# Layer statistics on TensorE: each 32-column block sums its own 128 tokens, turned within PSUM, without a fold

## Chip, cores, metric

One core of a Trainium2 chip. The metric is device time in microseconds (us), where smaller is better. A run counts as slow when it is over 1.5% above the fastest run of the same kernel; all comparisons of times below use fast runs.

The engines go by these names: PE is TensorE (matmul), PEld its weight loads, DVE is VectorE, ACT is ScalarE, POOL is GpSimd, SP is SyncE. PSUM is where TensorE writes its results, in banks. The granted clock is the share of TensorE's full clock that it gets. A column tile is a strip of 32 of TensorE's 128 columns that is used as a small unit with its own weights; how TensorE is split for a group of matmuls is its tiling mode.

## The reference

```python
kv  = einsum('bhsd,bhse->bhde', k, v)          # 8 batches, 8 heads, 576 tokens, 64
o   = einsum('bhsd,bhde->bhse', q, kv)
x   = o / sqrt(mean(o*o, -1) + 1e-6) * g_norm  # -> 4608 tokens x 512
h   = x @ w_in                                 # 512 -> 1024
u   = h * exp(h) / sum(exp(h))                 # the maximum that it subtracts cancels out
out = (u - mean(u)) / sqrt(var(u) + 1e-6) * g_ln @ w_out
```

The mean and the variance of `u` are over the 1024 features of one token. The kernel keeps features on partitions, so these sums run across partitions, and it does them on TensorE.

## The kernel before

The tokens are taken in nine chunks (0 to 8) of 512. Per chunk the kernel makes `h` (8 groups of 4 matmuls), `e = exp(h)` on ACT, `u = h*e` on DVE, `usq = u*u` on POOL or ACT, `es` (sums of pairs of `e`) on POOL, then three sums per token, from them the factor `rstd`, and `out` (8 groups of 4 matmuls), which DVE scales by `rstd` into `ob` and SP stores. The attention part of later batches (kv, qT, o, s) lies in between.

These are the parts concerned:

```python
banks = {"h": 2, "out": 2, "o": 2, "s": 1, "misc": 1}          # PSUM banks by name

def sums(c, part):                       # 20 matmuls of 512 columns on four 32-column tiles
    if part == 0:
        T["sum", c] = bank(("misc" if c else "h", "sum", c), [128, 512], FP32)
    i, src = ((1, T["u", c]), (0, T["usq", c]), (2, T["es", c]))[part]
    n_src = NF // 2 if part == 2 else NF
    for n in range(n_src):
        j = n % 4
        nc.tensor.matmul(
            T["sum", c][32 * j:32 * j + 32, :], stat_sel[:, i, :], src[:, n, :],
            start=(part == 0 and n < 4), stop=(part == 2), tile_position=(0, 32 * j), ...)

def sums_turn(c):                        # 32x32 blocks turned by DVE, PSUM to SBUF
    t = T["sumT", c] = tile_of(("sumT", c), [128, 4, 4, 32], FP32)
    nc.vector.transpose(t.rearrange("p a b c -> p (a b c)"), T["sum", c][:, :])

def stats_mm(c):                         # the fold: adds the four partial sums
    t = T["st", c] = bank(("misc", "st", c), [128, 4, 3], FP32)
    for g in range(4):
        nc.tensor.matmul(t[32 * g:32 * g + 32, :, :], fold[:, :], T["sumT", c][:, :, g, 0:3],
                         start=True, stop=True, tile_position=(0, 32 * g))
# (cut) stats: three small DVE operations -> vare; rstd: Ln and Exp on ACT
```

Each of the four column tiles adds two of the eight feature blocks (of `es` one of four) for all 512 tokens. So four partial sums exist, and the fold, four fp32 matmuls (eight in the records), adds them after the turn.

The order of all work is not written by hand. Every piece is entered into a plan with an estimated length and the pieces it needs, and the plan issues it greedily:

```python
plan.add(("turn", c), "dve", 0.62, ..., [("sums", c)], ...)
plan.add(("st_mm", c), "pe", 0.15, ..., ["fold", ("turn", c)], ...)
plan.add(("stats", c), "dve", 0.65, ..., [("st_mm", c)], ...)
plan.add(("rstd", c), "act", 0.45, ..., [("stats", c)])
# (cut) ... and at the end:
for fn in plan.order():
    fn()
```

Each engine gets its pieces in that order. A change of one piece's length can therefore reshuffle the whole program.

The softmax here doesn't subtract the row's maximum and nothing guards it: scores larger than these inputs give would overflow.

## Time and profile before

| | before |
|---|---|
| median of 3 runs | 199.07 us (198.79 to 199.22) |
| span of the profiled run | 196.4 us |
| TensorE busy | 180.7 us, 92% |
| sums of chunk 0, 3, 8 start at | 35.99, 101.77, 185.33 us |
| from the end of sums to the start of scaling, chunk 5 | 136.21 to 138.93 us |

The prediction shows the page and the windows.

I use the start of each chunk's sums as milestones. The work of TensorE between two of them (chunk 0 to 3, and 3 to 8) is the same in both orders, apart from the statistics: I counted the groups in the issue lists (27 h and 23 out groups in the first stretch, 37 and 40 in the second).

### The profile page before, as it was taken

The page shows a single profiled execution, that of the slowest core. Times are in us where ns is not written, and L with a number is a line of the kernel's source. Part 1 is how long each engine was busy: PE and PEld are TensorE (multiplying, and loading weights), DVE is VectorE, ACT ScalarE, POOL GpSimd, SP SyncE. Part 2 cuts the span into 40 slices and gives each one's busy share as a digit, 9 for nine tenths or more (in the row PEclk, how much of TensorE's full clock was granted, in tenths as well). Part 3 has the DMA queues.
Part 4 walks back from the last instruction along what each step waited for, and adds up shares of the span by engine and source line. Part 5 has one row for each costly group of instructions (what it writes and reads, how often), then busy time and mean ns, then how long its engine had stood idle before and what let it go on. Part 6 is the DMA issues. An engine that isn't in the chain of part 4 may idle for free.

```text
span 196.4 us, 4455 instructions
## 1 busy us (share of the span) xinstructions
PE 180.7 (92%) x1780; PEld 83.2 (42%) x1806; DVE 126.0 (64%) x244; ACT 140.3 (71%) x244; POOL 128.8 (66%) x137
## 2 busy tenths in 40 slices
PE   7997988779999989999999999999999999999990
PEld 2442455335444434445444443444454444344430
DVE  2465687466867595678667957767584667665350
ACT  2038877886987899888889697888879296546421
POOL 7982699501899876987898684679193828835200
PEclk9999999969999999999999999999999999999997
DMA  4999999999995999899799965362112011211206
GB/s 50 196 203 298 323 203 204 202 208 245 218 235 87 151 193 239 169 154 235 124 141 244 218 118 186 110 132 86 53 53 86 25 65 48 104 53 71 94 15 198
DMA packets 35893, 29.65 MB, mean 151 GB/s; under 512 B 11801, under 2 KB 30241, under 8 KB 35873
## 3 DMA queue, kind: packets, MB, share of 16 engines
q0 software_dynamic: 20112, 17.30, 55.3%
q1 hardware_dynamic: 15472, 11.54, 19.9%
q10 hardware_dynamic: 288, 0.52, 0.9%
q8 instruction: 14, 0.23, 0.5%
q14 instruction: 7, 0.05, 0.1%
HBM read 32.51 MB, written 9.44 MB: 214 GB/s over the span
## 4 chain that ended last, share of the span: by engine, by line
PE 73%; DMA 11%; POOL 5%; ACT 4%; DVE 3%; issue 2%; POOLq 0%
PE out_ps L595 28%; PE h_ps L474 26%; DMA q_sb<-in_q_dram 7%; PE misc_ps L538 5%; DMA v_sb<-in_v_dram 3%; PE o_ps L354 3%; PE s_ps L375 3%; PE o_ps L595 2%; PE misc_ps L297 2%; POOL usq_sb L500 2%; DVE u_sb L489 1%; POOL k_sb L223 1%; PE misc_ps L198 1%; PE misc_ps L325 1%; DVE x_sb L396 1%
## 5 line engine op out<-in xcount | busy, mean ns | idle before, releaser
L474 PE MATMUL h_ps<-x_sb,w_in_sb 128*128 128x512 bf16 x267 | 68.8, 379 | 2.2 <-DVE x_sb L396 1.1
L595 PE MATMUL out_ps<-w_out_sb,u_sb 128*128 128x512 bf16 x257 | 67.1, 383 | 2.8 <-issue 1.2
L500 POOL TENSOR_TENSOR usq_sb<-u_sb 128x512 bf16<-128x512 bf16 x51 | 52.8, 1041 | 24.3 <-DVE u_sb L489 24.1
L506 POOL TENSOR_TENSOR es_sb<-e_sb 128x512 bf16<-128x512 f32 x36 | 45.7, 1272 | 25.8 <-ACT e_sb L482 25.5
L489 DVE TENSOR_TENSOR u_sb<-h_ps,e_sb 128x512 bf16<-128x512 f32 x69 | 47.2, 688 | 23.6 <-ACT e_sb L482 23.1
L482 ACT ACTIVATE e_sb<-h_ps,zero_t 128x512 f32<-128x512 f32 x69 | 47.0, 683 | 11.9 <-PE h_ps L474 11.6
L474 PEld LDWEIGHTS <-w_in_sb 128*128 128x128 bf16 x288 | 27.0, 98 | 34.7 <-issue 4.3
L595 PEld LDWEIGHTS <-u_sb 128*128 128x128 bf16 x288 | 26.9, 99 | 34.7 <-issue 6.5
L605 DVE TENSOR_SCALAR ob_sb<-out_ps,rstd 128x512 f32<-128x512 f32 x33 | 24.6, 747 | 12.0 <-PE out_ps L595 6.5
L396 DVE SCALAR_TENSOR_TENSOR x_sb<-o_ps,g_rep,rst_sb 128x512 bf16<-128x512 f32 x32 | 23.9, 749 | 9.5 <-ACT rst_sb L383 9.4
L369 ACT ACTIVATE osq_sb<-o_ps,zero_t 128x512 bf16<-128x512 f32 x31 | 19.8, 682 | 11.3 <-PE o_ps L354 11.1
L383 ACT ACTIVATE rst_sb<-lss_sb,zero_t 128x512 f32<-128x512 f32 x32 | 23.2, 726 | 0.6
L379 ACT ACTIVATE lss_sb<-s_ps,eps_t 128x512 f32<-128x512 f32 x32 | 22.0, 686 | 0.4 <-PE s_ps L375 0.4
L498 ACT ACTIVATE usq_sb<-u_sb,zero_t 128x512 bf16<-128x512 bf16 x21 | 15.1, 720 | 8.1 <-DVE u_sb L489 7.9
L375 PE MATMUL s_ps<-osq_sb,head_mean 128*128 128x512 bf16 x34 | 13.2, 387 | 0.9 <-ACT osq_sb L369 0.8
L198 PE MATMUL s_ps<-zeros 128*128 128x512 bf16 x27 | 9.9, 492 | 1.6 <-DVE zero_t L163 1.2
L223 POOL DMA_DIRECT2D k_sb<-in_k_dram x10 | 7.9, 786 | 3.8 <-DMA w_in_sb<-in_moe_w_in_dram 2.3
L231 POOL DMA_DIRECT2D q_sb<-in_q_dram x10 | 8.6, 857 | 1.6 <-DMA w_in_sb<-in_moe_w_in_dram 1.4
L572 ACT ACTIVATE lv<-vare,zero_t 128x4 f32<-128x4 f32 x9 | 2.7, 299 | 9.5 <-DVE vare L568 9.5
L315 DVE CAST kvd<-misc_ps 64x128 bf16<-64x128 f32 (+1 forms) x24 | 6.9, 288 | 3.1 <-PE s_ps L297 1.7
L354 PE MATMUL o_ps<-qT_sb,kvd 64*64 64x32 bf16 (+1 forms) x240 | 8.3, 256 | 0.2 <-ACT qT_sb L332 0.2
L297 PEld LDWEIGHTS <-k_sb 64*64 64x64 bf16 x576 | 6.7, 107 | 3.8 <-issue 3.8
(83 smaller groups left out, 140.1 us busy)
## 6 DMA issues: line engine op xcount, KB each, us to landing
out_dram<-ob_sb SPq DMA_DIRECT2D x34, 256.0 KB, 3.6
k_sb<-in_k_dram POOLq DMA_DIRECT2D x6, 576.0 KB, 12.8
v_sb<-in_v_dram POOLq DMA_DIRECT2D x6, 576.0 KB, 12.9
q_sb<-in_q_dram POOLq DMA_DIRECT2D x6, 512.0 KB, 14.7
w_out_f<-in_moe_w_out_dram POOLq DMA_DIRECT2D x1, 2048.0 KB, 15.9
k_sb<-in_k_dram POOLq DMA_DIRECT2D x4, 288.0 KB, 11.1
v_sb<-in_v_dram POOLq DMA_DIRECT2D x4, 288.0 KB, 11.8
q_sb<-in_q_dram POOLq DMA_DIRECT2D x4, 256.0 KB, 11.8
```

Of the source, the lines that this page charges most:

```text
L369: nc.scalar.activation(out=t[:, :], in_=T[("o", *i)].rearrange("p a b c -> p (a b c)"), func=AF.Square, bias=zero_t[:, :])
L375: nc.tensor.matmul(t[:, :], head_mean[:, :], T["osq", i][:, :], start=True, stop=True)
L379: nc.scalar.activation(out=t[:, :], in_=T["s", i][:, :], func=AF.Ln, bias=eps_t[:, :])
L383: nc.scalar.activation(out=t.rearrange("p a b c -> p (a b c)"), in_=T["lss", i][:, :], func=AF.Exp, scale=-0.5, bias=zero_t[:, :])
L396: nc.vector.scalar_tensor_tensor(out=T["x", c][:, 2 * hf:2 * hf + 2, z], in0=T["o", c, hf, z][:, :, :, :], scalar=g_rep[:, :], in1=T["rst" ...
L474: nc.tensor.matmul(t[:, :], w_in_sb[:, dt, f * 128:(f + 1) * 128], T["x", c][:, dt].rearrange("p a b c -> p (a b c)"), start=(dt == 0), st ...
L482: nc.scalar.activation(out=T["e", c, f // 2][:, f % 2, :], in_=T["h", c, f][:, :], func=AF.Exp, bias=zero_t[:, :])
L489: nc.vector.tensor_tensor(out=T["u", c][:, f, :], in0=T["h", c, f][:, :], in1=T["e", c, f // 2][:, f % 2, :], op=MUL)
L500: nc.gpsimd.tensor_tensor(out=dst, in0=src, in1=src, op=MUL)
L506: nc.gpsimd.tensor_tensor(out=T["es", c][:, n, :], in0=e[:, 0, :], in1=e[:, 1, :], op=ADD)
L595: nc.tensor.matmul(T["acc", c, m][:, :], T["u", c][:, f, m * 128:(m + 1) * 128], w_out_sb[:, f, :], start=(f == 0), stop=(f == NF - 1),)
L605: nc.vector.tensor_scalar_mul(out=t[:, :], in0=T["acc", c, m][:, :], scalar1=T["rstd", c][:, m:m + 1])
```

## The change

The intent: give each column tile its own tokens, so that its sum is complete and no fold is needed. Tile j takes of every 128 tokens the 32 of block j. After the turn of 32x32 blocks, now from PSUM into the same PSUM bank, tokens lie on partitions as wanted.

```diff
-                tiling = n[0] if n[0] in ("kv_mm", "o_mm", "sums", "st_mm") else "full"
+                tiling = n[0] if n[0] in ("kv_mm", "o_mm", "sums") else "full"
 ...
-            T["sum", c] = bank(("misc" if c else "h", "sum", c), [128, 512], FP32)
+            T["sum", c] = bank(("misc" if c else "h", "sum", c), [128, 2, 128], FP32)
 ...
-            j = n % 4
-            nc.tensor.matmul(
-                T["sum", c][32 * j:32 * j + 32, :], stat_sel[:, i, :], src[:, n, :],
-                start=(part == 0 and n < 4), stop=(part == 2), tile_position=(0, 32 * j), skip_group_check=True,
-            )
+            for j in range(4):
+                cols = src[:, n, :].rearrange("p (m j r) -> p j m r", m=4, j=4)[:, j]
+                nc.tensor.matmul(
+                    T["sum", c][32 * j:32 * j + 32, 0, :], stat_sel[:, i, :], cols, start=(part == 0 and n == 0),
+                    stop=(part == 2 and n == n_src - 1), tile_position=(0, 32 * j), skip_group_check=True,
+                )
 ...
-        t = T["sumT", c] = tile_of(("sumT", c), [128, 4, 4, 32], FP32)
-        nc.vector.transpose(t.rearrange("p a b c -> p (a b c)"), T["sum", c][:, :])
-    def stats_mm(c): ...   (the fold, cut)
+        T["st", c] = T["sum", c][:, 1, :].rearrange("p (m i) -> p m i", m=4)
+        nc.vector.transpose(T["sum", c][:, 1, :], T["sum", c][:, 0, :])
 ...
-        plan.add(("turn", c), "dve", 0.62, ...)
-        plan.add(("st_mm", c), "pe", 0.15, ...)
+        plan.add(("turn", c), "dve", 0.25, ...)
```

The set-up of `fold` is gone as well. Because the turn's length and the piece `st_mm` are gone from the plan, the order of issue changes: above all between the sums of chunk 0 and chunk 3. I call the statistics "old" and "new", and likewise the order.

More of the change, by code (lines that the diff above doesn't have):

```diff
@@ L126 @@
         "k": 3, "v": 3, "q": 3, "qT": 3, "osq": 4, "lss": 2, "rst": 2, "oc": 2, "x": 2, "e": 4, "u": 2, "usq": 2, "es": 2,
-        "sumT": 2, "ob": 4,
+        "ob": 4,
     }
@@ L156 @@
     eye = big.tile([NF, NF], FP32, name="eye")
-    fold = big.tile([128, 32], FP32, name="fold")
     zeros = big.tile([128, 512], BF16, name="zeros")
@@ L208, in make_ident @@
         make_identity(nc, eye)
-    def make_fold():
-        for j in range(4):
-            nc.vector.tensor_copy(fold[32 * j:32 * j + 32, :], ident[32 * j:32 * j + 32, 32 * j:32 * j + 32])
     plan.add("ident", "pool", 1.0, -1.95, make_ident)
-    plan.add("fold", "dve", 1.0, 0.2, make_fold, ["ident"])
     def load_kv(name, src, b, hs):
@@ L536, in sums @@
         for n in range(n_src):
-            j = n % 4
-            nc.tensor.matmul(
-                T["sum", c][32 * j:32 * j + 32, :], stat_sel[:, i, :], src[:, n, :],
-                start=(part == 0 and n < 4), stop=(part == 2), tile_position=(0, 32 * j), skip_group_check=True,
-            )
-    def sums_turn(c):
-        t = T["sumT", c] = tile_of(("sumT", c), [128, 4, 4, 32], FP32)
-        nc.vector.transpose(t.rearrange("p a b c -> p (a b c)"), T["sum", c][:, :])
-    def stats_mm(c):
-        t = T["st", c] = bank(("misc", "st", c), [128, 4, 3], FP32)
-        for g in range(4):
-            nc.tensor.matmul(
-                t[32 * g:32 * g + 32, :, :], fold[:, :], T["sumT", c][:, :, g, 0:3],
-                start=True, stop=True, tile_position=(0, 32 * g),
-            )
+            for j in range(4):
[4 more added lines that the diff above has]
+                )
+    def sums_turn(c):
+        T["st", c] = T["sum", c][:, 1, :].rearrange("p (m i) -> p m i", m=4)
+        nc.vector.transpose(T["sum", c][:, 1, :], T["sum", c][:, 0, :])
     small = ctx.enter_context(tc.tile_pool(name="small", bufs=2))
@@ L565, in stats @@
         terms = small.tile([128, 4, 3], FP32, name="terms")
-        nc.vector.tensor_tensor(out=terms[:, :, :], in0=st[:, :, :], in1=w[:, :, :], op=MUL)
+        nc.vector.tensor_tensor(out=terms[:, :, :], in0=st[:, :, 0:3], in1=w[:, :, :], op=MUL)
         T["vare", c] = small.tile([128, 4], FP32, name="vare")
@@ L624 @@
                  uses=[("u", c), ("usq", c), ("es", c)], first=[("misc" if c else "h", "sum", c)])
-        plan.add(("turn", c), "dve", 0.62, rs + 0.14, lambda c=c: sums_turn(c), [("sums", c)],
-                 uses=[("misc" if c else "h", "sum", c)], first=[("sumT", c)])
-        plan.add(("st_mm", c), "pe", 0.15, rs + 0.15, lambda c=c: stats_mm(c), ["fold", ("turn", c)],
-                 uses=[("sumT", c)], first=[("misc", "st", c)])
-        plan.add(("stats", c), "dve", 0.65, rs + 0.16, lambda c=c: stats(c), [("st_mm", c)], uses=[("misc", "st", c)])
+        plan.add(("turn", c), "dve", 0.25, rs + 0.14, lambda c=c: sums_turn(c), [("sums", c)],
+                 uses=[("misc" if c else "h", "sum", c)])
+        plan.add(("stats", c), "dve", 0.65, rs + 0.16, lambda c=c: stats(c), [("turn", c)], uses=[("misc" if c else "h", "sum", c)])
         plan.add(("rstd", c), "act", 0.45, rs + 0.17, lambda c=c: rstd(c), [("stats", c)])
```

## The prediction

> **What bounds the kernel now.** I read the page first: busy shares and the slices of the span.
>
> ```profile
> span 196.4 us, 4455 instructions
> PE 180.7 (92%) x1780; PEld 83.2 (42%) x1806; DVE 126.0 (64%) x244; ACT 140.3 (71%) x244; POOL 128.8 (66%) x137
> ...
> PE   7997988779999989999999999999999999999990
> ...
> PEclk9999999969999999999999999999999999999997
> ```
>
> TensorE is the bound, but not everywhere: its digits are full only from about slice 10 (49 us). The table of windows says where it is not full:
>
> ```profile
> 28.00:34.00 6.00, 4.36 (x89) 2.92 (x83) 4.97 (x8) 4.63 (x10) 5.97 (x7) 1.00 1.27 205
> 34.00:40.00 6.00, 4.22 (x53) 1.88 (x51) 2.64 (x7) 5.11 (x9) 2.94 (x4) 1.00 1.32 203
> 40.00:46.00 6.00, 4.76 (x90) 2.83 (x93) 3.76 (x7) 3.62 (x9) 0.00 (x0) 0.72 1.20 222
> 46.00:66.00 20.00, 19.61 (x276) 9.66 (x278) 14.32 (x27) 16.74 (x31) 15.94 (x16) 1.00 1.05 183
> 66.00:86.00 20.00, 18.84 (x131) 7.78 (x133) 15.43 (x31) 18.35 (x33) 16.75 (x17) 1.00 1.08 188
> ```
>
> Columns: window, length, busy of PE, PEld, DVE, ACT, POOL, clock, DMA share, GB/s. From 28 to 46 us TensorE idles 4.7 us of 18, and in the last third of it the granted clock is 0.72. After 46 us it is 94 to 99% busy, so there every TensorE microsecond removed is worth about one. From 66 to 86 us ACT is 92% busy: it is close behind.
>
> So two things matter: TensorE time per chunk of 512 tokens in the full part, and what the order of work does in the hole at 34 to 46 us. The timeline of one chunk's statistics:
>
> ```profile
> 135.02 0.77 PEld L538 LDWEIGHTS <-stat_sel 128*32 128x32 bf16 x20 [0.42 <-issue]
> 135.02 0.61 PE L538 MATMUL misc_ps<-u_sb,stat_sel 128*32 128x512 bf16 x8
> ...
> 136.21 0.55 PEld L595 LDWEIGHTS <-u_sb 128*128 128x128 bf16 x4 [0.42 <-issue]
> ...
> 136.34 0.71 DVE L547 STREAM_TRANSPOSE sumT_sb<-misc_ps 128x512 f32<-128x512 f32 x1
> ...
> 137.18 0.16 PEld L552 LDWEIGHTS misc_ps<-sumT_sb,fold 128*32 128x32 f32 x8 [0.42 <-DVE sumT_sb L547]
> ...
> 137.36 0.55 PEld L474 LDWEIGHTS <-w_in_sb 128*128 128x128 bf16 x4
> ```
>
> The sums take 135.02 to 136.21 = 1.19 us until the next group loads. Four output matmuls at 0.216 us then end at 137.07; the fold starts at 137.18 (0.11 us of switching) and the next group at 137.36 (0.18 us). The fold thus takes 0.29 us of TensorE. At 104.27, 155.96 and 187.50 I find the same 0.18 us, and 0.11 to 0.13 ahead of it.
>
> **What the Trainium skill says.** "TensorEngine Tiling (Array Packing)", Key Properties: tiles of one mode run independently, and changing the mode drains TensorE. The trace agrees: 20 sums matmuls of 512 columns take 1.19 us, five rounds of four at 0.216 plus 0.11, and each change of tiling costs about 0.1 us. "TensorE: Matmul & The Clock Gate", Back-to-back issue gap, gives 134 cycles for N=128 and 518 for N=512 at 2.4 GHz, so four short ones cost about 4% more than a long one; the same page (Part 1) has starts never closer than about 25 ns. The trace contradicts this floor for packed tiles: the kv matmuls (64x64 quadrants, 64 columns, each with its weight load) put 72 pairs into 61.93 to 62.51 us, 8 ns a pair. Part 1 also says that an idle TensorE falls back to half clock; the 0.72 above agrees.
>
> **The change part by part.**
> Sums: 20 matmuls of 512 columns become 80 of 128, still 10,240 columns over four column tiles, each tile now always on its own 128 tokens. Stream: 20 rounds of four at 134 cycles (55.8 ns, an estimate from the clock gate page) = 1.12 us against 1.08. Issue: 80 pairs at 8 ns = 0.64 us, hidden under it. Weights: the fold's eight fp32 pairs of 32 weight columns went at 0.18/8 = 22 ns, often two in a row on one tile, so a load fits in a 56 ns round. Expected 1.23 us per chunk, +0.04. I chose the streaming bound.
> Fold: gone, -0.29 us per chunk. Chunks 1 to 8 lie in the full part: 8 x (0.29 - 0.04) = **2.0 us saved**.
> Turn: the transpose shrinks from 128x512 (0.71 us) to 128x128; taking some 0.17 us fixed (the small DVE operations of the statistics last 0.16 to 0.17), I estimate 0.17 + 0.54/4 = 0.31. DVE drops by 9 x 0.4 = 3.6 us and the fold's set-up copies (0.9 us), but it is 64% busy: worth nothing directly. Variance is known about 1 us earlier, as no TensorE turn stands in between; that frees out banks sooner.
> Banks: the sums now stay in their bank until the statistics are read, instead of until the turn; the second tenancy of misc for the fold's result goes. About even.
>
> Order: here the change does more than its diff. The recorded order of the two programs shows TensorE and its helpers reshuffled between sums(0) and chunk 3. Before: sums(0), fold, o(1,1), s, qT(2), s, 8 out, kv(2), h(1). After: sums(0), kv(2), o(1,1), 8 out, s, qT(2), 4 out, s, qT(2), o(2,0), 4 out, s, h(1). In the trace before, this part reads:
>
> ```profile
> 38.42 0.41 PE L354 MATMUL h_ps<-qT_sb,kvd 64*64 64x256 bf16 x8
> 39.62 0.38 PE L375 MATMUL s_ps<-osq_sb,head_mean 128*128 128x512 bf16 x1 [0.78 <-ACT osq_sb L369]
> 40.86 1.03 PE L325 MATMUL misc_ps<-ident,q_sb 128*128 128x128 bf16 x8 [0.86 <-DMA q_sb<-in_q_dram]
> 41.69 0.63 PE L375 MATMUL s_ps<-osq_sb,head_mean 128*128 128x512 bf16 x1
> 42.11 0.63 PE L595 MATMUL out_ps<-w_out_sb,u_sb 128*128 128x512 bf16 x1
> ```
>
> TensorE is nearly empty from 37.1 to 40.9 us, waits for q of batch 2 and then works cold. After, kv(2) and 8 output matmuls fill that gap. By hand from these durations: kv(2) to 37.9 (if v of batch 2 is there), o(1,1) from 38.3 (its second h bank comes free after statistics), 8 out to 40.5, q lands at 40.86 as before, qT to 41.3, 4 out, s at 42.2; ln, exp and x end at 44.8, so h(1) starts near 45.0, against 45.6. Besides those 0.6 us, 8 out (1.7), qT (0.45), o (0.5) and s (0.2) are already done: a lead of **about 3.4 us**. I don't count it whole. The filler is spent: h(1) with the work in between is some 10.5 us of TensorE, while ACT then has 8 exp (5.5), two osq (1.3), four ln and four exp (5.6) and copies (0.8) = 13.2 us, so ACT holds TensorE up. Followed to the start of h(2), I have it at about 59.5 us instead of 63.1, but with 8 out matmuls and one kv (2.5 us) still owed: a lead of **about 1.1 us**, and perhaps 0.2 more where 66 to 86 us now has filler.
>
> Sum: 2.0 + 1.1 + 0.2 = 3.3 us; 199.07 - 3.3 = 195.8. The tail (last output block, its scaling and store) is unchanged.
>
> **The rivals.**
> (a) Sums slower than their stream. For: the moving operand is read in four runs of 32 columns, and the o matmuls of the last chunk, whose 32 columns are strided, take 1.06 us for 64 pairs (16.5 ns, double kv's). Against: those are steps of 8 elements, here 32 neighbours lie together. At 80 ns a round: +0.5 us per chunk, 8 x 0.5 = 4 us, so about 200.
> (b) The early hoist hits a DMA: TensorE takes its work in order, so kv(2) ahead of o(1,1) blocks it until v lands; kv(3) and qT(3), needed from about 47 and 50 us instead of 56 and 52, may do so too. For: DMA share is 1.2 to 1.3 there and q of batch 2 took 14.4 us to land. Against: v was issued at 24.6 us, 1.8 ahead of that q. A loss of 1 to 3 us would leave only the fold: 197 to 199.
> (c) The lead survives whole, because out matmuls postponed refill later gaps and the clock never falls: 3.4 + 2.0 = 5.4 us, 193.7. Against: ACT at 92% from 66 to 86 us.
> (d) Only the fold counts, order being a wash: 197.1.
>
> **Range and chances.** I take 195.9, between the sum and (d), with 193.9 to 198.0: the lower end is nearly (c), the upper (b) with the fold's gain half kept. Two per cent faster is 195.1, inside the range on the good side: 0.32. Slower by 2% (203) needs (a) at twice its size and (b) together: 0.03.
>
> **What would show each step.** Sums' first start to the next group's load: 1.2 to 1.3 us (over 1.5 means rival a). No fold matmuls; TensorE busy down by about 2 us or, where short pairs are counted differently, at least no new idle after 70 us. Turn near 0.31 us. At 37 to 41 us TensorE full instead of nearly empty, clock above 0.9 from 40 to 46 us, h(1) near 45 and h(2) near 59.5 us. Waits of kv or qT on k, v or q above 1 us would speak for (b); TensorE waiting for ACT's exp in h(1) for the shrunken lead. I am wrong if the sums cost what they save, or if the early order and not the fold carries the whole difference.

## More of the kernel before

One more stretch is needed later: the timeline of before for chunk 5, after the fold (start, duration, engine, line, operation, out<-in, shapes; in brackets the idle time ahead and what ended it).

```profile
138.27 0.30 ACT L572 ACTIVATE lv<-vare,zero_t 128x4 f32<-128x4 f32 x1 [1.31 <-DVE vare L568]
138.60 0.30 ACT L574 ACTIVATE rstd<-lv,zero_t 128x4 f32<-128x4 f32 x1
```

ACT stood still for 1.31 us until DVE had the variance.

## The result

The changed kernel took 196.25 us (median of 4 runs, 195.25 to 196.85), the kernel before 199.12 us in the same rounds. The ratio is 0.9854, 95% interval 0.9806 to 0.9901: within 2%, but faster. A ratio is the mean time of one kernel's fast runs over that of the other's in the same rounds, so it isn't quite the ratio of the medians.

The page of the changed kernel:

```profile
span 193.5 us, 5420 instructions
PE 179.4 (93%) x2274; PEld 87.9 (45%) x2274; DVE 122.2 (63%) x240; ACT 140.8 (73%) x244; POOL 129.0 (67%) x137
...
PE   7799896979799989999999999999999999999990
...
PEclk9999999999999999999999999999999999999999
```

The clock never falls now (before, one digit was a 6, and the last one, where TensorE has run out of work, a 7), and the span is 2.9 us shorter while TensorE's busy time is only 1.3 us shorter. The windows, in the columns of the prediction:

```profile
28.00:34.00 6.00, 4.45 (x99) 2.93 (x97) 5.93 (x10) 4.57 (x10) 5.96 (x7) 1.00 1.27 205
34.00:40.00 6.00, 5.24 (x180) 3.44 (x179) 2.35 (x8) 5.63 (x11) 3.88 (x5) 1.00 1.31 202
40.00:46.00 6.00, 5.26 (x42) 2.79 (x42) 5.03 (x10) 4.77 (x10) 0.00 (x0) 1.00 1.20 226
46.00:66.00 20.00, 18.39 (x183) 8.57 (x185) 14.42 (x24) 18.50 (x33) 16.12 (x17) 1.00 1.10 186
66.00:86.00 20.00, 19.18 (x323) 9.49 (x324) 14.32 (x31) 16.71 (x32) 17.52 (x18) 1.00 1.24 204
```

From 34 to 46 us TensorE is busy 10.5 us instead of 9.0, and at full clock. In the next 20 us it is less busy than before (18.39 against 19.61), with ACT at 18.50 of 20: some of the lead seems to be given back there.

The timeline of the changed kernel, for chunk 5's statistics:

```profile
133.31 0.63 PE L533 MATMUL misc_ps<-u_sb,stat_sel 128*32 128x128 bf16 x32
...
134.55 1.04 PE L581 MATMUL out_ps<-w_out_sb,u_sb 128*128 128x512 bf16 x4
...
134.67 0.33 DVE L541 STREAM_TRANSPOSE misc_ps<-misc_ps 128x128 f32<-128x128 f32 x1
...
135.42 1.03 PE L467 MATMUL h_ps<-x_sb,w_in_sb 128*128 128x512 bf16 x4
...
135.65 0.30 ACT L558 ACTIVATE lv<-vare,zero_t 128x4 f32<-128x4 f32 x1 [0.40 <-DVE vare L554]
135.98 0.30 ACT L560 ACTIVATE rstd<-lv,zero_t 128x4 f32<-128x4 f32 x1
```

The sums take 133.31 to 134.55 = 1.24 us, the turn 0.33 us, and no fold follows. From the end of the sums to the end of `rstd` it is 1.73 us, before it was 2.69 us (136.21 to 138.90). ACT waits 0.40 us instead of 1.31 us.

Where the 2.9 us of span came from, by milestones:

| stretch | before | changed | changed, profiled again (a0) |
|---|---|---|---|
| start to sums of chunk 0 | 35.99 | 36.94 | 37.18 |
| sums 0 to sums 3 | 65.78 | 63.62 | 64.29 |
| sums 3 to sums 8 | 83.56 | 82.29 | 82.29 |
| sums 8 to the end | 11.07 | 10.65 | 10.64 |

The first row goes the wrong way, and is chance: sums 0 began between 36.6 and 37.4 us in all thirteen later profiles, whichever code they had, so the 35.99 of before is the outlier. The difference is there from the second kv group on, which started at 12.05 us in before and between 12.48 and 13.17 us in the others (the first one, at 7.77 us and 7.56 to 8.71 us, does not tell them apart). So the gain comes from two places: 1.5 to 2.2 us from chunk 0 to 3, and 1.7 us after that.

### The profile page after: what moved, and what is told of

Its sections match the earlier page's. It is cut to its first block, busy times and chain, and to the rows that moved or that the text cites. A ratio compares the mean times of both kernels' runs of the same rounds, so it can differ in the third digit from the quotient of the medians.

```text
span 193.5 us, 5420 instructions
## 1 busy us (share of the span) xinstructions
PE 179.4 (93%) x2274; PEld 87.9 (45%) x2274; DVE 122.2 (63%) x240; ACT 140.8 (73%) x244; POOL 129.0 (67%) x137
## 4 chain that ended last, share of the span: by engine, by line
PE 64%; DMA 23%; POOL 7%; issue 1%; ACT 1%; DVE 1%; POOLq 0%
PE out_ps L581 25%; PE h_ps L467 24%; DMA q_sb<-in_q_dram 11%; DMA qT_sb<-q_sb 8%; PE misc_ps L533 4%; DMA v_sb<-in_v_dram 4%; PE o_ps L347 3%; PE s_ps L368 3%; POOL usq_sb L493 2%; PE o_ps L581 2%; POOL k_sb L216 2%; POOL v_sb L216 1%; PE misc_ps L197 1%; POOL es_sb L499 1%; POOL q_sb L224 1%
## 5 line engine op out<-in xcount | busy, mean ns | idle before, releaser
L467 PE MATMUL h_ps<-x_sb,w_in_sb 128*128 128x512 bf16 x276 | 70.0, 379 | 1.7 <-DVE x_sb L389 1.1
L581 PE MATMUL out_ps<-w_out_sb,u_sb 128*128 128x512 bf16 x272 | 68.6, 379 | 1.5 <-DVE ob_sb L591 1.1
L475 ACT ACTIVATE e_sb<-h_ps,zero_t 128x512 f32<-128x512 f32 x69 | 47.3, 685 | 10.5 <-PE h_ps L467 10.1
L533 PEld LDWEIGHTS <-stat_sel 128*32 128x32 bf16 x720 | 10.1, 97 | 3.7 <-issue 3.2
L290 PE MATMUL misc_ps<-v_sb,k_sb 64*64 64x64 bf16 x360 | 7.7, 194 | 2.0 <-DMA v_sb<-in_v_dram 2.0
```

What stands on the lines that cost most here:

```text
L467: nc.tensor.matmul(t[:, :], w_in_sb[:, dt, f * 128:(f + 1) * 128], T["x", c][:, dt].rearrange("p a b c -> p (a b c)"), start=(dt == 0), st ...
L475: nc.scalar.activation(out=T["e", c, f // 2][:, f % 2, :], in_=T["h", c, f][:, :], func=AF.Exp, bias=zero_t[:, :])
L581: nc.tensor.matmul(T["acc", c, m][:, :], T["u", c][:, f, m * 128:(m + 1) * 128], w_out_sb[:, f, :], start=(f == 0), stop=(f == NF - 1),)
```

## The experiments

Theory: the saving is TensorE's time for the fold, 0.25 us per chunk, and the new order adds a lead in the thinly filled stretch ("the hole", 37 to 46 us). Rivals: the order alone does it; or the fold cost little itself and the shorter way to the statistics counts; or the hoisted loads cost something that hides a larger gain.

For runs with a foreign order, the plan's order was printed as a list and issued from it, with `st_mm` taken out, or put in one TensorE group after its turn. All runs gave correct results, with five rounds each.

### a0: the changed kernel again

No edit. 

> The changed kernel once more, as the control that the other runs of this call are compared with. Both theories: ratio 0.985 to the kernel before, 196.2 us. Its first kv matmuls started 0.9 us later than before in the first profile (8.63 against 7.77 us); if that is chance of the first loads, some profile of this or the next runs shows 7.8 us; if it belongs to the longer program, both kernels with the 80 short matmuls show about 8.6 us and the others 7.8.

196.42 us, ratio 0.9885 (0.9844 to 0.9927). The gain repeats, about 2.3 us by the means. The steady stretch repeats to the hundredth (82.29).

### a1: new statistics, old order

```diff
-    for fn in plan.order(): fn()
+    for n in ORDER: plan.pieces[n][3]()     # the order of before without st_mm; stats of chunk 0 one o group earlier
```

> The new statistics (80 short matmuls, no fold) issued in the order of the kernel before; only the statistics of chunk 0 move ahead of one o group. Theory (the fold costs 0.25 us of TensorE per chunk net, the order brings the rest): 2.0 us faster than before, 197.1, ratio 0.990. Rival (the order carries the whole difference): 199.1, ratio 1.000.

198.36 us, ratio 0.9999 (0.9959 to 1.0039): nothing gained. Chunks 3 to 8 took 82.58 us, so the fold's time is saved there (1.0 us). It was lost in the hole: sums 0 to 3 took 67.82 us against 65.78. The timeline of a1 shows one cause:

```profile
39.98 0.41 PE L480 MATMUL h_ps<-qT_sb,kvd 64*64 64x256 bf16 x7 [1.85 <-DVE terms L685]
```

The first chunk's sums lie in an h bank. Old statistics free it at the turn; new ones only when `terms` has been read, and in this order DVE did other work first. TensorE stood for 1.85 us, and then had half clock from 41.8 to 48.6 us. This profile is of the longest of a1's six runs (199.38 us, mean clock 0.977); the four with a mean clock of 0.989 to 0.991 took 197.83 to 198.40 us.

### a2: old statistics, new order

The same kind of edit in the kernel before, with the order of the changed kernel. 

> The old statistics (20 long matmuls, wide turn, fold) issued in the order of the changed kernel; fold and statistics stand one TensorE group after the turn. Theory: 1.0 to 1.3 us faster than before, about 197.9, ratio 0.994. Rival (only the fold counts, the order is a wash): 199.1, ratio 1.000. Second rival (the order's lead of 3.4 us is kept whole): 195.7, ratio 0.983.

203.56 us, ratio 1.0257 (1.0213 to 1.0302): far slower, and outside all three forecasts. So the order is no gain by itself. ACT's wait for the variance (`lv` waiting for `vare` in the tables of waits) was in all:

| before | changed | a2 |
|---|---|---|
| 9.5 us | 5.5 us | 17.8 us |

ACT reaches `rstd` at the time that suits the short chain, finds no variance and stands.

### a3: before, with the fold done twice

```diff
-        for g in range(4):
+        for g in (0, 1, 2, 3, 0, 1, 2, 3):
```

> The kernel before, with each fold's four matmuls issued twice into the same result (0.18 us more TensorE time per chunk, no more switching, the same order). Theory (TensorE is the bound in chunks 1 to 8): 8 x 0.18 = 1.4 us slower, 200.5, ratio 1.007. Rival (TensorE has slack there and the fold's cost is the wait for the turn): within 0.3 us of before, ratio 1.000 to 1.002.

199.57 us, ratio 1.0064 (1.0012 to 1.0117). The timeline of a3:

```profile
139.19 0.31 PE L552 MATMUL misc_ps<-sumT_sb,fold 128*32 128x12 f32 x16
139.44 1.04 PE L474 MATMUL h_ps<-x_sb,w_in_sb 128*128 128x512 bf16 x4
```

From fold to next group it is now 0.25 us, before 0.18. Eight more recorded matmuls cost 0.07 us, and chunks 3 to 8 became 0.33 us longer (83.89): 0.066 per chunk. I had expected 0.18. So the matmuls of the fold are a quarter of its 0.29 us. The rest, about 0.22 us, I put down to coming into its tiling mode and out of it; that is argued, since no small group in the mode of its neighbours was run. In the means the total rose by 1.3 us. Nine folds at 0.066 us are 0.6 us or 0.3%, which the interval holds. That the total lies at the 1.007 of the theory is then chance.

### b1: a1 with the bank freed early

```diff
-    ('turn', 0), ('ex', (1, 0, 1)), ('x', (1, 0, 1)), ('stats', 0), ('o_mm', 1, 1),
+    ('turn', 0), ('stats', 0), ('ex', (1, 0, 1)), ('x', (1, 0, 1)), ('o_mm', 1, 1),
```

> As a1, but the statistics of chunk 0 stand straight after its turn on VectorE, so that the bank of the sums comes free before the o group asks for it. In a1 that group waited 1.85 us longer, TensorE fell to half clock from 42 to 48 us, and the 0.2 us per chunk won later were lost there. Theory (fold alone, hole as before): 2.0 us faster than before, ratio 0.990; sums of chunk 3 to sums of chunk 8 about 82.3 us against 83.6. Rival (the bank held longer is part of the change and can't be had without the new order): ratio 1.000 again.

198.42 us, ratio 1.0013 (0.9960 to 1.0066). The wait for the bank fell from 1.85 to 0.64 us, sums 0 to 3 took 66.26 us (a1: 67.82), yet no gain shows in total. The bank was not the cause, or not alone. The windows of b1, two us each:

```profile
38.00:40.00 2.00, 0.99 (x36) 0.52 (x25) 1.49 (x6) 1.61 (x3) 0.11 (x1) 1.00 1.41 200
40.00:42.00 2.00, 0.38 (x1) 0.00 (x0) 0.61 (x2) 1.97 (x5) 0.00 (x0) 1.00 1.24 209
42.00:44.00 2.00, 1.73 (x13) 0.94 (x14) 2.00 (x4) 1.56 (x4) 0.00 (x0) 0.80 1.21 206
44.00:46.00 2.00, 2.00 (x6) 0.56 (x4) 0.90 (x2) 0.59 (x1) 0.00 (x0) 0.50 1.25 215
46.00:48.00 2.00, 2.00 (x78) 1.25 (x78) 0.77 (x3) 0.72 (x3) 0.00 (x0) 0.84 1.17 283
```

From 38 to 42 us TensorE is idle for 2.6 of 4 us. Then the clock falls, and it is at half just where TensorE has work in plenty (2.00 of 2.00). Before has its low clock earlier, from 40 to 44 us, with less work under it (1.14 and 1.78 of 2). From the shares 0.80 and 0.84 I work out, as an estimate with half clock as the only other state, that b1's clock was low from about 43.2 to 46.6 us. That gave a new theory: in the old order the hole costs the clock, and what the fold's removal saves is paid there.

### b2: a2 with the statistics later on DVE

In a2 DVE took `stats` directly behind the fold; here the pieces of DVE's that stood ready go ahead of it. 

> As a2, but the small VectorE operations stand one more TensorE group later, as in the kernel before. In a2 VectorE waited 9.3 us in all for the fold's result and the chunks 3 to 8 took 86.4 us instead of 83.6. Theory (the new order by itself gains 1 to 1.5 us up to chunk 3 and nothing after): ratio 0.993 to 0.995, chunks 3 to 8 about 83.6 us. Rival (the new order doesn't suit a fold at all: VectorE blocked again): ratio above 1.01.

204.05 us, ratio 1.0274 (1.0239 to 1.0309): no better, so DVE waiting for the fold was not what made a2 slow. ACT's wait remains, as the timeline of b2 shows for chunk 5:

```profile
141.38 0.30 ACT L706 ACTIVATE lv<-vare,zero_t 128x4 f32<-128x4 f32 x1 [2.02 <-DVE vare L702]
```

### b3: before, with the hole filled

```diff
+    plan.add(("fill", 0), "pe", 0.9, 9.0, lambda: warm(4, "misc"))   # 128x512 matmuls on zeros,
+    plan.add(("fill", 1), "pe", 0.7, 9.0, lambda: warm(3, "s"))      # results never read
+    plan.add(("fill", 2), "pe", 0.9, 9.0, lambda: warm(4, "misc"))
+    # order: sums 0, fill 0, fold, o(1,1), fill 1, s, fill 2, qT(2)
```

> The kernel before in its own order, with 11 idle matmuls on zeros put into the hole between 37 and 41 us (4 after sums of chunk 0, 3 after the o group, 4 after the first s), results never read. Theory (a good part of the order's gain is that the clock does not fall): granted clock 1.0 from 40 to 46 us instead of 0.72, the 8 output matmuls there in 1.7 us instead of 2.6, 1.0 to 1.4 us faster than before, ratio 0.994. Rival (the clock is hidden behind the waits for q and ACT): ratio 1.000.

198.11 us, ratio 0.9969 (0.9931 to 1.0007): at most a small gain, the interval just reaches 1. The clock stayed at 1.00 from 40 to 46 us, and sums 0 to 3 took 64.42 us, 1.36 us less than before. In before TensorE was busy for 2.83 of the 3.41 us at half clock (40.50 to 43.91 us); half of that, 1.4 us, is an estimate of what it lost. In total less shows, perhaps because two of before's ten fast runs in these rounds kept their clock (0.995).

### b4: the changed kernel with later loads

kv(3) moved back behind the third h group of chunk 1, and qT(3) behind the fifth, so that v and q have more time to land. 

> The changed kernel with kv of batch 3 moved behind the next h group and the first turn of q of batch 3 behind another h group, so that they no longer stand in front when v and q are still on their way (0.6 and 0.7 us of waiting in its profile). Theory (those waits stand beside ACT's own delay in this stretch): 0 to 0.5 us faster than the changed kernel, ratio to before 0.983 to 0.986. Rival (the hoist costs its waits in full): 1.3 us faster than the changed kernel, ratio 0.979.

196.03 us, ratio 0.9885 (0.9842 to 0.9928), the same as a0. In the changed kernel kv(3) waited 0.60 us for v and qT(3) 0.67 us for q (0.43 and 1.46 us in a0). Here neither waits, and nothing came of it: what these two waits cost is too small for this comparison. The wait of kv(2), 0.77 us here, was not taken away.

### c1 and d1: new statistics, old order, hole filled

The order of b1 with the eleven fillers of b3. 

> The changed kernel's statistics in the order of the kernel before (as in b1), with the same eleven filler matmuls as in b3 in TensorE's idle stretch after the first chunk's sums. Theory (in the old order the saving of the fold was lost because TensorE stood idle there and its clock fell): clock 1.0 in 40 to 46 us, first three chunks (sums of chunk 0 to sums of chunk 3) about 64.5 us against 66.3 in b1, chunks 3 to 8 82.6 us as in b1, ratio to the kernel before about 0.990, equal to the changed kernel within 0.3%. Rival (the new order carries more than the clock, for instance because chunk 1's work is fitted in beside chunk 0's statistics): ratio 0.995 or more, first three chunks over 65.3 us.

196.4 us, ratio 0.9862 (0.9792 to 0.9932). As the profile fell on a slow run, it was run again as d1. It was run on another chip. 

> The same kernel as c1 once more, because the profile of c1 fell on a run of the slow state (a wait of 4 us for a store and a load near 112 us). Theory (new statistics in the old order are worth as much as the whole change once TensorE's clock is kept up in the idle stretch): fast runs 195.5 to 196.8 us, ratio 0.985 to 0.990 to the kernel before, sums of chunk 0 to sums of chunk 3 about 64.6 us, chunks 3 to 8 82.6 us in a fast profile. Rival (c1's ratio was luck of its rounds, since b1 without the filler gave 1.001): ratio 0.995 or more.

197.23 us, ratio 0.9871 (0.9834 to 0.9907) by its four fast runs (195.42 to 197.90). Both ratios lie at that of the changed kernel, although the order is the old one. The windows of c1, to be held against b1:

```profile
40.00:42.00 2.00, 1.58 (x7) 0.41 (x5) 0.56 (x1) 1.94 (x5) 0.00 (x0) 1.00 1.25 211
42.00:44.00 2.00, 1.84 (x15) 1.14 (x16) 2.00 (x4) 1.66 (x3) 0.00 (x0) 1.00 1.21 206
44.00:46.00 2.00, 2.00 (x79) 1.08 (x78) 1.37 (x4) 0.94 (x3) 0.00 (x0) 1.00 1.25 215
```

The clock stays up, and the same eight out matmuls show what it is worth (b1, then c1):

```profile
42.95 3.35 PE L714 MATMUL out_ps<-w_out_sb,u_sb 128*128 128x512 bf16 x8
42.83 1.89 PE L719 MATMUL out_ps<-w_out_sb,u_sb 128*128 128x512 bf16 x8
```

The fillers do no work early, and the o group ended at 39.6 us in both, yet h(1) started at 45.36 us against 47.09 in b1. Sums 0 to 3 took 64.61 and 64.52 us, against 66.26 in b1. That is 1.65 to 1.74 us less; half of b1's 3.4 us at half clock, all of them busy, is 1.7 us. A stall spoils what follows in these two profiles, which are both of slow runs; sums 0 to 3 lie ahead of it. In c1:

```profile
114.27 0.27 PE L485 MATMUL o_ps<-qT_sb,kvd 64*64 64x256 bf16 x1 [1.64 <-DMA qT_sb<-q_sb]
116.69 0.64 PE L485 MATMUL o_ps<-qT_sb,kvd 64*64 64x256 bf16 x7 [2.15 <-DVE x_sb L527]
```

TensorE loses some 4 us near 112 us to a late transposing load, while DVE waits 4.8 us for a store; d1 has it at the same place, with 3.8 us. In c1 the clock falls to half behind it, from 116.6 to 120.0 us. Four of the 13 runs of c1 and d1 were slow, against one of 12 of a0 and b4 together. Why this kernel meets the stall more often was not looked into. It is no better kernel than the changed one.

### c2: old statistics, new order, `rstd` later on ACT

b2 with ACT's two instructions for `rstd` one piece later in chunks 1 to 7. 

> The old statistics (with the fold) in the new order, as in b2, but with ScalarE's two instructions for rstd in chunks 1 to 7 put one piece of work later. Theory (b2 was slow because ScalarE, in order, stood for 2.0 us per chunk at a variance that the longer chain brings late): the wait per chunk falls by about 0.7 us or more, chunks 3 to 8 take 83.6 to 84.5 us instead of 86.4, ratio to the kernel before 1.000 to 1.010. Rival (it is not ScalarE's wait but VectorE's or the banks' places in the new order): chunks 3 to 8 stay at 86 us, ratio 1.025.

202.78 us, ratio 1.0209 (1.0150 to 1.0267). ACT's wait for the variance fell from 18.7 to 6.3 us in all, but chunks 3 to 8 took 85.5 us, only 0.9 of the 2.8 us that b2 has above before. So my theory holds for a third of that stretch. The rest of the loss is spread over TensorE's h, out and kv groups, and stays open.

### c3: the changed kernel with a fold that does nothing

```diff
+    # one group after each sums, into the bank that this group then overwrites; nobody reads it
+    for g in range(4):
+        nc.tensor.matmul(t[32 * g:32 * g + 32, 0:12], idle_w[:, :], idle_w[:, 0:12],
+                         start=True, stop=True, tile_position=(0, 32 * g))
```

> The changed kernel, complete and correct, with a meaningless fold put back one group of TensorE after each chunk's sums: four fp32 128x32 matmuls on constants, nobody waits for their result. Theory (what the steady gain of 0.25 us per chunk consists of is TensorE's time for the fold): 0.29 us more per chunk, chunks 3 to 8 from 82.3 to about 83.7 us, span 2.3 us longer than the changed kernel's, ratio to the kernel before about 0.998. Rival (the fold's price was the longer way to the statistics, not TensorE's time): at most 0.3 us in the whole, ratio 0.988.

199.49 us, ratio 1.0021 (0.9952 to 1.0089): the gain is gone. Chunks 3 to 8 took 83.61 us instead of 82.29: 1.32 us for five folds, 0.26 each. The timeline of c3:

```profile
137.87 1.04 PE L603 MATMUL out_ps<-w_out_sb,u_sb 128*128 128x512 bf16 x4
138.84 0.25 PE L473 MATMUL h_ps<-idle_w 128*32 128x12 f32 x8
139.02 1.04 PE L486 MATMUL h_ps<-x_sb,w_in_sb 128*128 128x512 bf16 x4
```

From this out group to the h group it is 1.15 us; in the changed kernel 0.87 us (134.55 to 135.42). The difference of 0.28 us is the fold's price with nobody waiting for it. By the means of fast runs 2.6 us were lost in all (a0 -2.25, c3 +0.39), which is about nine times 0.28. The profiled run lost 3.3 us of span against a0's (194.4 to 197.7). Of these, 2.2 us lie between sums 0 and 3, more than three folds: chunk 1's idle fold met a stall of its own there, TensorE stood 1.45 us in the midst of its matmuls, for nothing that the profile names. So it is the 0.26 us per steady chunk that is shown, and the total agrees. The theory's 2.3 us was near; the rival's 0.3 us is out.

### The four corners together

By the means of fast runs, in us against before in the same rounds (by the intervals of the ratios each is uncertain by 0.7 to 1.4 us):

| | old order | old order, hole filled | new order |
|---|---|---|---|
| old statistics | 0 | -0.6 (b3) | +5.0 (a2), +5.4 (b2), +4.1 (c2) |
| new statistics | 0.0 (a1), +0.2 (b1) | -2.9 (c1), -2.5 (d1) | -2.3 (a0), -2.4 (b4) |

With the hole filled, the statistics bring 1.8 to 2.3 us. In the old order as it was they bring nothing. The new order brings as much as the filler does, and not more.

Before's own runs point the same way. In the interleaved runs, those with a mean clock of 0.992 or more took 197.25 to 197.94 us (five fast runs, mean 197.56); those with 0.985 to 0.988 took 198.04 to 200.08 us (26 runs, mean 199.03). The same program thus keeps its clock in some runs and loses it in others, and the difference is of the size that is at stake.

## Why the prediction was right

- **Sums, +0.04 us per chunk.** Measured 1.24 and 1.23 us against 1.19. The choice of the streaming bound was right (57 ns a round of four, by the 16 rounds from 36.94 to 37.85 us, against the estimate of 55.8; the page gives that gap for matmuls without their weight loads, but the loads did not show here), and rival (a), slow columns in four runs of 32, was not seen.
- **Fold, -0.29 us.** Right: 0.26 to 0.28 when put back alone (c3). That its matmuls are only 0.07 of it (a3) the prediction did not say, though its own 0.11 us ahead of the fold hinted at it.
- **Turn, 0.31 us.** Measured 0.33. "Variance is known about 1 us earlier": 2.69 to 1.73 us.
- **Chunks 1 to 8, 2.0 us.** The step is right per chunk: (83.56 - 82.29) / 5 = 0.25 us. It does not hold for all eight. From chunk 3 to the end it gave 1.27 + 0.42 = 1.7 us. In the filled old order, sums 0 to 3 took 64.42 us with old statistics (b3) and 64.6 us with new ones (c1, d1): no gain from the earlier chunks. There ACT is near its limit (92% in 66 to 86 us), but I did not test that as the cause.
- **The lead of the order.** This is the step that was wrong in its parts. "h(1) starts near 45.0, against 45.6" (45.76 by its first matmul); it started at 46.73. h(2), expected near 59.5, started at 60.21 (before: 63.32), so there was a lead. The working let 8 out matmuls follow o(1,1) and end at 40.5. The changed kernel's timeline:

```profile
39.26 0.41 PE L347 MATMUL h_ps<-qT_sb,kvd 64*64 64x256 bf16 x8
40.74 1.89 PE L581 MATMUL out_ps<-w_out_sb,u_sb 128*128 128x512 bf16 x8 [1.07 <-DVE ob_sb L591]
42.47 0.38 PE L368 MATMUL s_ps<-osq_sb,head_mean 128*128 128x512 bf16 x1
```

  The out matmuls waited 1.07 us for a bank, which DVE frees by scaling, and scaling waits for chunk 0's statistics. They ended at 42.5, 2 us late; 0.95 us of it is the later start by chance. "That frees out banks sooner" was in the text, but the wait itself was not in the sum.
- **Banks, "about even".** In the new order nothing waits for the bank of chunk 0's sums. In the old order the o group behind them waited 1.85 us (a1) and 0.64 us (b1), which the kernel before does not show.
- **What the order is worth.** 1.1 + 0.2 us predicted; the stretch from sums 0 to 3 became 1.5 to 2.2 us shorter. The size is near, the reason given was not the main one. It spoke of work done early; the clock was only a thing to be checked ("clock above 0.9": it was 1.00). c1 and d1 show that idle matmuls in the old order, which do no work early at all, give the same total. Keeping TensorE busy through the hole, and so its clock up, is what counts.
- **The sum, 3.3 us.** Measured 2.9 us in the first rounds, 2.3 and 2.4 us in a0 and b4. It is near in part by luck: the fold gave 1.7 us instead of 2.0, and as much as the order gave can be had in the old order by keeping the clock up (c1, d1), which had no term in the sum.
- **Rival (d), the fold alone, 197.1 us.** Not what happens: the new statistics in the old order gave 198.4 us (a1, b1). "Order being a wash" was wrong for this pair, since in that order the clock is lost where there is work.
- **Rival (b), loads.** kv(2), kv(3) and qT(3) did wait, 0.43, 0.60 and 0.67 us (0.38, 0.43 and 1.46 in a0). b4, without the last two waits, is no faster.
- **Rival (c), the whole lead.** Not seen; from 46 to 66 us TensorE was less busy than before, with ACT 92% busy, as the prediction feared.
- **DVE's savings "worth nothing directly".** True for its busy time. But the new order pays only with the new statistics: with the old ones it costs 4.1 to 5.4 us (a2, b2, c2). The prediction treated the order as a bonus beside the change; it fits the change only.

What stays open: why the old statistics in the new order lose more than ACT's wait for the variance; the stall near 112 us in c1 and d1; and where b1 loses all it saved. Of the 2.6 to 3.1 us between b1 and c1 or d1, 1.65 to 1.74 us is seen in sums 0 to 3. Two of b1's six runs had a mean clock of 0.975 and 0.976 and took 199.76 and 200.09 us; the other four, at 0.989 to 0.991, lie 0.4 us below before. With these alone 2.0 to 2.5 us are to be explained, and the rest is within the intervals.

## What to carry to other kernels

A tiny matmul group between groups of another tiling mode cost far more than its arithmetic (0.22 of 0.29 us here were not its matmuls, and probably its two mode changes), so count groups, not matmuls. When part of a kernel has an idle stretch of a few microseconds on TensorE, ask what it does to the clock of the work behind it: a saving elsewhere can vanish there, and a dozen idle matmuls can bring it to light. And where a planner orders the work, test calculation and order apart, since each may be worthless without the other.

## What the Trainium skill lacked or had wrong

- "TensorE: Matmul & The Clock Gate", "Wait — 56ns, not 53.3ns?", has starts of matmuls never closer than about 25 ns, however few columns they have. Said like that it is too wide, for on packed tiles they are closer, as the page itself allows further on: 80 sums matmuls of 128 columns on four column tiles, each with its weight load, took 1.23 to 1.24 us, so 15.4 ns a pair of load and matmul, and 72 pairs of kv on 64x64 quadrants took 0.58 us, 8 ns a pair.
- The same page gives the idle time after which the clock halves (about 3.4 us), but not how little work holds it up. In the 14 profiles here the recorded clock changes only at steps of 3.41 us. I laid such steps over each profile and read TensorE's busy time in each. Wherever it was 1.51 us or less, the next step had half clock (before 1.13 us in 37.09 to 40.50, b1 1.31, b2 1.51); wherever it was 1.62 us or more, the clock stayed up (after sums 0 the least were 1.90 us, in a2 and c3; c1 had 3.36).
- "TensorEngine Tiling (Array Packing)", "Key Properties", says that a change of mode drains TensorE, but gives no price. Here a detour of four fp32 128x32 matmuls between two 128x128 groups cost 0.26 to 0.29 us (c3, before), of which the matmuls themselves were 0.07 us (a3). How much of the rest is the drain was not measured apart.
- "VectorE: DVE Perf Modes", "The three transpose paths", lists VectorE's transpose as going to SBUF, with 311 ns for 128x128 bf16. It also goes from PSUM into the same PSUM bank: 128x128 f32 in 0.33 us.
